# Second bucket pass of a graph-hop kernel: first hop in runs of 3, 3, 3 pairs, three small copies on ScalarE

## The chip, the cores and the metric

One core of one Trainium2 chip. The metric is the device time of one execution in microseconds (us), the median of several runs. One execution was also taken with the hardware profiler; the trace rows below are of that one.

## The reference

N = 10000 nodes, E = 160000 directed edges with random ends, D = 128 features. Seven rounds ("hops") of normalised neighbour sums give eight tokens per node, which then go through one small attention block and a weighted readout.

```python
h = x; toks = [x]
for _ in range(7):
    msg = h[src] * deg_inv_sqrt[src, None] * deg_inv_sqrt[dst, None]
    h = segment_sum(msg, dst, N)
    toks.append(h)
tok = stack(toks, axis=1)                    # (N, 8, D)
# layernorm, self-attention over the 8 tokens, residual, readout softmax -> (N, D)
```

## The kernel before, in words

The 10000 nodes are cut into 79 tiles of 128. A hop multiplies one-hot matrices with the table of node values, so the edges must first be sorted into cells by destination tile and source block. Stages, in order of time: a first bucket pass over the edge list (`pass_a`, to about 400 us of the trace), `decode`, the **second bucket pass** (about 400 to 1160 us), which makes the one-hot matrices tile by tile and runs the first hop with them as they come, then hops 2 to 7 from the stored matrices, then the attention.

The change is in the second bucket pass (`run`, L657 to L725). It goes over 20 groups of four tiles, called quads here (the code's `quads`). In each round of the loop at L706 three generators are advanced in turn, so that their instructions are written out mixed:

- `place(quad q+1)` (L418 to L504), mostly VectorE (DVE) and TensorE (PE). The quad's four tiles are done two at a time: one-hot of the cell keys `oh` (L213), counts on PE (L430, L436) with two ScalarE (ACT) casts `H` and `U` (L431, L438), the product `ux` (L226), ranks `rk` on PE and DVE (L230 to L234), the rank's one-hot `rob` (L213), two products `R` (L219), 50 matmuls `tb` (L449), the cast `tbs` on ACT (L450). Once per quad there follows the overflow part: `dsl` (ACT, L467), `oidx` (L468), `fl`, `ct`, `po`, the overflow ranks `ph` (L483), the digits of the overflowing edges, two one-hots `ohp` (L213) with 16 small matmuls each into `msc` (L496), the copy `lo` of the result (L499), `oidx` again (L502) and `Sov` (L503).
- `matrices(quad q)` (L506 to L536): per tile, rows `rb` and `ra` are fetched from DRAM by the SP queue (L517), and the one-hot tile `w` is built in three parts: L524 on DVE from `rb`, two L529 on ACT from `ra`, L532 on DVE from `dsl`; then `w` is stored to DRAM (`gsd`, L534). `rb` has one buffer, `ra` two, `w` six.
- `hop1(quad q-1)` (L697 to L701) through `block` (L548 to L638): per tile 9 pairs of gathers. One gather is 8 matmuls of 32 columns into a PSUM tile `p` (L608, three buffers); ACT copies it out as `eb` (L613; in the last quad DVE does four of the nine, L615). The copied pair is summed into the PSUM tile `acc` by four matmuls (L558, L559, "scatter"), which are written out two pairs behind the gathers (`lag` is 2). `runs` says how many gathers are written out before the scatters that are due: (2, 2, 2, 3) before. At the tile's end come the two rows of fetched values (`og`, by POOL's indirect DMAs) and a ones column (L566), which close the tile, and then `fin1` (L676): the in-degree `indeg` copied from column 128 of `acc` (L677), `y` and `r` scaled from `acc` on ACT (L680, L651), and every second tile `tab` and `mx`, and the stores.

The order on an engine is not the order of the code alone: a list scheduler in the build reorders each engine's instructions, with the code's order as priority, and sets the semaphores. An engine then runs its list strictly in order. Two buffers matter below: `ux` and `R` share one buffer (tag `ux`, one copy), so the next `ux` waits until `tb` has read `R`; `ohp` and `rob` share one as well.

Of the kernel before, what the change touches and what calls it, by code (L numbers as in the profile page):

```python
# [12 lines left out]
AF = mybir.ActivationFunctionType  # L13
ALU = mybir.AluOpType
# [22 lines left out]
KO = 8  # L37
# [10 lines left out]
class Hops:  # L48
# [369 lines left out]
    def place(self, ts, got):  # L418

        tc, nc, V, A, T, G = self.tc, self.nc, self.nc.vector, self.nc.scalar, self.nc.tensor, self.nc.gpsimd  # L420
        wp, w1, n = self.bwp, self.bw1, len(ts)
# [34 lines left out]
        n, a, b = len(ts), ts[0], ts[-1] + 1  # L456
        msc = self.psm.tile([128, 128], F32, name="msc")
# [12 lines left out]
        n = 4  # L470
# [8 lines left out]
        po = wp.tile([128, 4, 8], F32, name="po")  # L479
        V.tensor_tensor(po[:, :n], msc[:, 0:n, None].to_broadcast([128, n, 8]), self.iof1[:, None, :8].to_broadcast([128, n, 8]), op=ALU.add)  # L480
        V.tensor_mul(po[:, :n], po[:, :n], fl[:, :n])
        ph = wp.tile([128, KO, 4], F16, name="ph")
        V.tensor_scalar(ph.rearrange("p k g -> p g k"), po[:, :n, :KO], -1.0, None, op0=ALU.add)  # L483
        vi = wp.tile([128, 4, 8, 4], I32, name="vi4")
        V.tensor_scalar(vi[:, :n, :, 3], ov[:, :n], -1.0, None, op0=ALU.add)
        V.tensor_single_scalar(vi[:, :n, :, 0], vi[:, :n, :, 3], 14, op=ALU.arith_shift_right)
# [9 lines left out]
                    T.matmul(msc[:, 4 + 3 * (g + i):7 + 3 * (g + i)], ohp[:, k, :, i], dg[:, g + i, k, :], start=k == 0, stop=k == KO - 1)  # L496
        yield
        lo = wp.tile([128, 16], F32, name="lo")
        V.tensor_copy(lo[:, :3 * n], msc[:, 4:4 + 3 * n])  # L499
        l3 = lo[:, :12].rearrange("p (g k) -> p g k", k=3)  # L500
        n = len(ts)
        V.scalar_tensor_tensor(self.oidx[:, a:b, NI], l3[:, :n, 0], 128.0, l3[:, :n, 1], op0=ALU.mult, op1=ALU.add)  # L502
# [154 lines left out]
    def run(self, ctx, att, nhop=K):  # L657
        tc, nc, V, A, T, G = self.tc, self.nc, self.nc.vector, self.nc.scalar, self.nc.tensor, self.nc.gpsimd
        with ExitStack() as c:
            self.bp = c.enter_context(tc.tile_pool(name="bp", bufs=1))  # L660
            self.TT = self.bp.tile([128, NCH, NTP], F32, name="TT")
            G.memset(self.TT[:, :, NK:], 0.0)
            self.pass_a()
            self.decode()
            self.gsp = c.enter_context(tc.tile_pool(name="gs1", bufs=6))
            self.pg = c.enter_context(tc.tile_pool(name="pg1", bufs=3, space=PSUM))
            self.pacc = c.enter_context(tc.tile_pool(name="pc1", bufs=2, space=PSUM))
            self.ogp = c.enter_context(tc.tile_pool(name="og1", bufs=2))
            self.fp = c.enter_context(tc.tile_pool(name="fp1", bufs=1))
            self.pb_open(c)  # L670
            pend = []

            done, stored = [], []


            def fin1(t, s, acc):  # L676
                V.tensor_copy(self.indeg[:, t:t + 1], acc[:, 128:129])  # L677
                if not done:
                    fin1.y = self.fp.tile([128, 2, 128], F32, name="y2")
                A.activation(fin1.y[:, len(done), :], s, AF.Copy, scale=self.dis2[:, t:t + 1])  # L680
                done.append(t)
                self.token_out(1, t, s, self.ctok[0])
                n, b = len(done), t + 1
                if n == 2 or b in (NT, 4 * NG):
                    a, new = b - n, self.tab[1]
                    self.to_table(fin1.y[:, :n, :], new, self.q2, a, b)
                    V.tensor_reduce(self.mx[1][:, a:b], new[:, a:b, 0:128], axis=X, op=ALU.max, apply_absolute_value=True)
                    stored.append((a, b))
                    done.clear()
                    while len(stored) > (t != last1):  # L690
                        self.rows(1, new, *stored.pop(0), nc.sync)


            quads = [list(range(a, min(NT, a + 4))) for a in (*range(4 * NG, NT, 4), *range(0, 4 * NG, 4))]
            dsl, W = [[] for _ in quads], [[] for _ in quads]

            def hop1(q):  # L697
                for t, w in zip(quads[q], W[q]):
                    og = [self.fetch(t, j, (self.tabd[0], self.tabh[0])) for j in range(NI + 1)]
                    yield from self.block(t, w, self.tab[0], og, pend, 2, (2, 2, 2, 3), True,  # L700
                                          lambda jj: q < nq - 1 or jj % 2 == 0, fin1, t == quads[0][0])  # L701

            nq, last1 = len(quads), quads[-1][-1]
            for _ in self.place(quads[0], dsl[0]):
                pass
            for q in range(nq + 1):  # L706
                pl = self.place(quads[q + 1], dsl[q + 1]) if q + 1 < nq else iter(())
                if q == 0:
                    mt = self.matrices(quads[0], dsl[0][0], W[0])
                    next(mt)  # L710
                hp = hop1(q - 1) if q else iter(())
                for i in range(16):
                    if i % 3 != 1:
                        next(pl, None)
                    if i % 4:
                        next(mt, None)
                    next(hp, None)
                for g in (pl, mt, hp):
                    for _ in g:
                        pass  # L720
                if q + 1 < nq:
                    mt = self.matrices(quads[q + 1], dsl[q + 1][0], W[q + 1])
                    next(mt)
            while pend:
                pend.pop(0)()  # L725
        with ExitStack() as c:
# [10 lines left out]
            pend = []  # L737
            for k in range(2, nhop + 1):
                i = 1 - k % 2
# [29 lines left out]
                og = [[None] * (NI + 1) for _ in order]  # L769
# [11 lines left out]
                for n, t in enumerate(order):  # L781
                    w = self.gsp.tile([128, (NJ + NG) * 128], F8, name="w")
# [591 lines left out]
```

## Time and profile before

| | us |
|---|---|
| median of 3 runs | 3912.85 (3900.72 to 3913.69) |
| profiled execution | 3935.55, of which 3933.8 are its span (mean granted TensorE clock 0.977) |
| second bucket pass | about 400 to 1160 of the span |
| the 20 `fl` (L473, one per quad): first start, last start | 403.7, 1099.0 |

The profiled execution is 22.7 us above the median of the runs. In the rows, "x" is a count, a "busy" share is the time in which an engine had an instruction in flight, and [0.88 <-PE tb L449] at a row's end says that the engine stood idle for 0.88 us before the instruction and that the end of PE's L449 released it. Neighbouring instructions of one engine overlap, so what an instruction costs its engine is the step from its start to the next one's start, and not its duration.

### The profile page before, as it was taken

Reading aid. Unit: us, or ns where it says so; the run is one execution under the profiler, and the core shown is the slowest. Engines: PE = TensorE matmul, PEld = TensorE weight load, DVE = VectorE, ACT = ScalarE, POOL = GpSimd, SP = SyncE. Lnnn points to the kernel's source line nnn. Section 1 sums busy time; section 2 is a strip of 40 time slices with the busy share of each in tenths; the row PEclk is TensorE's granted clock in tenths of the full one; section 3 lists DMA queues with packets and bytes.
Section 4 is the critical chain, followed back from the end, with each engine's and each line's share of the span. In section 5 each row is a group of like instructions: output and inputs, shape, how many; then the busy total and the mean of one; then the engine's idle time right before and its main releaser. Section 6 shows DMA issues by size and latency. Waiting matters only on the chain.

```text
span 3933.8 us, 174231 instructions
## 1 busy us (share of the span) xinstructions
PE 3693.9 (94%) x74141; PEld 2983.6 (76%) x74141; DVE 3172.3 (81%) x6888; ACT 2812.9 (72%) x6950; POOL 1678.8 (43%) x2221
## 2 busy tenths in 40 slices
PE   6786899999989999999999999999999998999997
PEld 4665677777768888888788788888878886777775
DVE  8998999999967777777777777777776664888888
ACT  6885577777766666766666667666765667888885
POOL 0000233323236665666666566656656662121111
PEclk8898899999999999999999999999999999999998
DMA  3100454544546666666666666666666552222220
GB/s 101 38 2 1 140 168 154 163 152 161 161 150 202 202 199 194 204 199 204 188 201 201 192 201 203 198 192 199 204 192 201 187 187 92 82 77 85 77 83 19
DMA packets 332729, 595.58 MB, mean 151 GB/s; under 512 B 57447, under 2 KB 215493, under 8 KB 326693
## 3 DMA queue, kind: packets, MB, share of 16 engines
q1 hardware_dynamic: 293989, 506.70, 40.0%
q0 software_dynamic: 35392, 72.55, 6.5%
q8 instruction: 580, 9.50, 1.0%
q10 hardware_dynamic: 2560, 5.12, 0.5%
q14 instruction: 208, 1.70, 0.1%
HBM read 455.49 MB, written 128.67 MB: 148 GB/s over the span
## 4 chain that ended last, share of the span: by engine, by line
PE 75%; DVE 14%; ACT 4%; DMA 4%; issue 2%; SPq 0%; another core or an unknown queue 0%; ACTq 0%; DVEq 0%; POOLq 0%
PE p L608 27%; PE acc L583 23%; PE acc L568 4%; PE pv L1018 4%; PE pu L1002 3%; DVE ux L226 2%; DVE o L219 2%; PE po L1037 2%; PE pt L992 2%; DVE oh L213 2%; PE tb L449 2%; DVE w L532 2%; PE ps L1067 1%; DVE R L219 1%; PE acc L558 1%
## 5 line engine op out<-in xcount | busy, mean ns | idle before, releaser
L613 ACT ACTIVATE eb<-p 128x512 f16<-128x512 f32 x3065 | 1638.7, 603 | 571.0 <-PE p L608 339.1
L615 DVE TENSOR_TENSOR eb<-p,four 128x512 f16<-128x512 f32 x1912 | 1230.9, 685 | 327.5 <-PE acc L583 189.7
L608 PE MATMUL p<-tab,w 128*32 128x256 f16 x39816 | 1291.8, 274 | 39.4 <-ACT eb L613 17.4
L608 PEld LDWEIGHTS <-w 128*32 128x32 fp8e4 x39816 | 997.5, 96 | 223.8 <-issue 169.2
L583 PE MATMUL acc<-eb,w 128*128 128x256 f16 x8532 | 1014.2, 273 | 0.5 <-issue 0.3
L583 PEld LDWEIGHTS <-w 128*128 128x128 fp8e4 x8532 | 836.9, 98 | 99.8 <-issue 1.0
L544 POOL DMA_INDIRECT og<-tabh,oidx x553 | 616.9, 1115 | 655.2 <-DVE oidx L468 394.5
L544 POOL DMA_INDIRECT og<-tabd,oidx x541 | 551.8, 1020 | 739.1 <-PE acc L566 359.6
L653 POOL TENSOR_SCALAR r<-s,ctok 128x128 f32<-128x128 f32 x474 | 294.8, 622 | 44.8 <-DVE s L599 27.8
L644 ACT ACTIVATE tab<-s,c 128x128 f16<-128x128 f32 x395 | 158.5, 401 | 198.0 <-DVE eb L615 171.4
L645 DVE SCALAR_TENSOR_TENSOR tab<-s,c,tab 128x128 f16<-128x128 f32 x395 | 138.9, 352 | 180.9 <-issue 168.3
L1107 POOL TENSOR_TENSOR p<-e,in 128x1024 f32<-128x1024 f32 (+1 forms) x40 | 76.5, 1914 | 446.6 <-DVE e L1106 446.6
L1059 ACT ACTIVATE junk<-tab 128x128 f32<-128x128 f32 x626 | 248.4, 401 | 8.2 <-SPq L1343 6.8
L347 ACT ACTIVATE rs<-iof,rb 128x128 fp8e4<-128x128 f32 x784 | 231.8, 391 | 0.3
L558 PE MATMUL acc<-eb,w 128*128 128x129 f16 x1422 | 214.2, 223 | 1.0 <-ACT w L529 0.9
L532 DVE TENSOR_TENSOR w<-dsl,iof 128x2432 fp8e4<-128x2432 f16 x79 | 211.9, 2682 | 2.7 <-PE acc L559 2.7
L599 DVE TENSOR_REDUCE s<-acc 128x128 f32<-128x256 f32 x474 | 196.3, 414 | 19.9 <-issue 8.9
L559 PE MATMUL acc<-eb,w 128*128 128x128 f16 x1422 | 210.1, 220 | 0.0
L543 POOL COPY og<-eb 128x1 f16<-128x1 f16 x452 | 84.0, 186 | 254.3 <-ACT eb L613 254.3
L558 PEld LDWEIGHTS <-w 128*128 128x128 fp8e4 x1501 | 139.2, 98 | 68.0 <-issue 64.3
L1018 PEld LDWEIGHTS pv<-Wv,xT 128*64 128x64 f32 x2504 | 138.8, 137 | 44.4 <-ACT uT L1003 29.7
L1018 PE MATMUL pv<-Wv,xT 128*64 128x131 f32 x2504 | 163.1, 280 | 8.6 <-issue 3.9
(299 smaller groups left out, 5033.1 us busy)
## 6 DMA issues: line engine op xcount, KB each, us to landing
w<-gsd SPq DMA_DIRECT2D x474, 592.0 KB
gsd<-w SPq DMA_DIRECT2D x79, 592.0 KB
tok<-r SPq DMA_DIRECT2D x546, 64.0 KB
tab<-tok SPq DMA_DIRECT2D x273, 128.0 KB
tabd<-tab SPq DMA_DIRECT2D x396, 64.0 KB
ra<-srow SPq DMA_DIRECT2D x79, 320.0 KB
rb<-srow SPq DMA_DIRECT2D x79, 256.0 KB
og<-tabh,oidx POOLq DMA_INDIRECT x553
```

The source lines that it names most:

```text
L347: A.activation(ro[:, j - a, i, :], self.iof, AF.Abs_reciprocal_sqrt, scale=2.0 ** 21, bias=rb[:, j - VP, i:i + 1], saturate=False)
L532: V.tensor_tensor(w[:, :NJ * 128].rearrange("p (j d) -> p j d", d=128), dsl[:, g, :, None].to_broadcast([128, NJ, 128]), self.iof1[:, None ...
L544: self.nc.gpsimd.indirect_dma_start(out=o, out_offset=None, in_=src[0] if i == NI else src[1], in_offset=bass.IndirectOffsetOnAxis(ap=self ...
L558: T.matmul(acc[0][:, :128 + ones], W, rows[:, 128:256 + ones], start=start, stop=False, skip_group_check=True)
L559: T.matmul(acc[0][:, :128], W, rows[:, :128], start=False, stop=False, skip_group_check=True)
L583: T.matmul(acc[0][:, :256], w[:, J * 128:(J + 1) * 128], e[:, j, :256], start=False, stop=J == NG - 1 and not late)
L608: T.matmul(p[32 * q:32 * q + 32, j], w[:, NJ * 128 + s * CAP:NJ * 128 + (s + 1) * CAP], tab[:, s, :], start=True, stop=True)
L613: A.activation(e[:, :n, 0:256], pv, AF.Copy, scale=4.0)
L615: V.tensor_tensor(e[:, :n, 0:256], pv, self.four[:, :, None].to_broadcast([128, n, 256]), op=ALU.mult)
L653: self.nc.gpsimd.tensor_scalar(r, s, ct[:, t:t + 1], None, op0=ALU.mult)
L1018: T.matmul(p[64 * h:64 * h + 64, u - us[0], :], S[i]["xT"][:, h * m + q, 64 * c:64 * c + 64], Wv, start=True, stop=True, tile_position=(0, ...
L1059: A.activation(j, S[i]["x"][:, g, :], AF.Square, bias=S[i]["x"][:, g, 0:1], scale=-1.0, accum_out=R[i % 6][:, 0, g:g + 1])
```

## The change

Four edits. The overflow ranks `ph` (once per quad), the overflow result `lo` (once per quad) and the in-degree column `indeg` (once per tile) go from DVE to ACT. The first hop's `runs` become (3, 3, 3), so a tile takes three rounds of the mixing loop and not four, and `hop1` is left out in every fourth round, so that it still spreads over the loop's 16.

```diff
-        V.tensor_scalar(ph.rearrange("p k g -> p g k"), po[:, :n, :KO], -1.0, None, op0=ALU.add)
+        A.activation(ph.rearrange("p k g -> p g k"), po[:, :n, :KO], AF.Copy, bias=-1.0)
...
-        V.tensor_copy(lo[:, :3 * n], msc[:, 4:4 + 3 * n])
+        A.copy(lo[:, :3 * n], msc[:, 4:4 + 3 * n])
...
             def fin1(t, s, acc):
-                V.tensor_copy(self.indeg[:, t:t + 1], acc[:, 128:129])
+                A.copy(self.indeg[:, t:t + 1], acc[:, 128:129])
...
-                    yield from self.block(t, w, self.tab[0], og, pend, 2, (2, 2, 2, 3), True,
+                    yield from self.block(t, w, self.tab[0], og, pend, 2, (3, 3, 3), True,
...
-                    next(hp, None)
+                    if i % 4 != 3:
+                        next(hp, None)
```

The lists of the engines are rebuilt by the scheduler, and they change in more places than the diff. Both builds come, after some quads, to a pattern that repeats from quad to quad; it is this pattern that is shown.

**Place 1**, DVE, the overflow part of a quad, from `oidx` (L468) on. Before:

```order
L468 TENSOR_SCALAR oidx<-msc 128x4
L532 TENSOR_TENSOR w<-dsl,iof_228 128x2432
L480 TENSOR_TENSOR po<-msc,iof_228 128x32
L524 TENSOR_SCALAR w<-rb,pid_232 128x1024
L481 TENSOR_TENSOR po<-po,fl 128x32
L483 TENSOR_SCALAR ph<-po 128x4x8
L213 TENSOR_TENSOR ohp<-ph,io_230 128x2048
L677 COPY indeg<-acc 128x1
L532 TENSOR_TENSOR w<-dsl,iof_228 128x2432
L213 TENSOR_TENSOR ohp<-ph,io_230 128x2048
```

The same place on DVE in the changed kernel:

```order
L468 TENSOR_SCALAR oidx<-msc 128x4
L532 TENSOR_TENSOR w<-dsl,iof_228 128x2432
L480 TENSOR_TENSOR po<-msc,iof_228 128x32
L524 TENSOR_SCALAR w<-rb,pid_232 128x1024
L481 TENSOR_TENSOR po<-po,fl 128x32
L532 TENSOR_TENSOR w<-dsl,iof_228 128x2432
L213 TENSOR_TENSOR ohp<-ph,io_230 128x2048
L165 SCALAR_TENSOR_TENSOR tab_65<-y_15189,q_252,tab_65 128x2x128
L687 TENSOR_REDUCE mx_249<-tab_65 128x2
L213 TENSOR_TENSOR ohp<-ph,io_230 128x2048
```

`ph` and `indeg` are gone, the second L532 of the quad stands ahead of the first `ohp` and not behind it, and between the two `ohp` there are now the short `tab` and `mx`. That L532 carries a new wait, for PE's scatters of an older tile whose `w` buffer it overwrites; before, the `indeg` on DVE ahead of it had already waited for the close of that tile or a later one.

**Place 2**, DVE, the middle of the same quad, from `Sov` (L503) to the next `ux` (L226), `R` being two rows. Before:

```order
L503 TENSOR_TENSOR Sov<-lo,iof_228 128x512
L677 COPY indeg<-acc 128x1
L524 TENSOR_SCALAR w<-rb,pid_232 128x1024
L532 TENSOR_TENSOR w<-dsl,iof_228 128x2432
L234 TENSOR_REDUCE rk<-ur 128x50
L213 TENSOR_TENSOR rob<-rk,io_230 128x1600
L452 SCALAR_TENSOR_TENSOR vo<-rk,TT 128x50
L219 TENSOR_TENSOR R<-rob,sl 128x25x64
L219 TENSOR_TENSOR R<-rob,dl 128x25x64
L454 MAX ov<-vo 128x8 x2
L524 TENSOR_SCALAR w<-rb,pid_232 128x1024
L213 TENSOR_TENSOR oh<-kB,io_230 128x3800
```

The same place in the changed kernel:

```order
L503 TENSOR_TENSOR Sov<-lo,iof_228 128x512
L524 TENSOR_SCALAR w<-rb,pid_232 128x1024
L532 TENSOR_TENSOR w<-dsl,iof_228 128x2432
L234 TENSOR_REDUCE rk<-ur 128x50
L524 TENSOR_SCALAR w<-rb,pid_232 128x1024
L213 TENSOR_TENSOR rob<-rk,io_230 128x1600
L452 SCALAR_TENSOR_TENSOR vo<-rk,TT 128x50
L219 TENSOR_TENSOR R<-rob,sl 128x25x64
L219 TENSOR_TENSOR R<-rob,dl 128x25x64
L454 MAX ov<-vo 128x8 x2
L226 TENSOR_TENSOR ux<-oh,U_15812 128x3800
```

The quad's third L524 moved up, from behind `R` to the place right behind `rk`, so only L532 and `rk` are left between it and the L524 ahead. Behind `R` there now comes `ux`, with nothing but the two MAX between; before, L524 and `oh` stood there. Both `oh` (before) and `ux` (now) wait at this place until PE's `tb` has read `R`.

**Place 3**, the SP queue, from the quad's second `rb` load to its third and fourth (L517). `tok` (L655) is the store of `r`, `gsd` (L534) that of `w`, `tabd` (L168) that of `tab`. Before:

```order
L517 DMA rb<-srow 128x1024
L655 DMA tok_66<-r 128x128
L534 DMA gsd_131<-w 128x4736
L517 DMA ra<-srow 128x1280
L168 DMA tabd_167<-tab_65 128x2x256
L517 DMA ra<-srow 128x1280
L655 DMA tok_66<-r 128x128
L517 DMA rb<-srow 128x1024
L534 DMA gsd_132<-w 128x4736
L517 DMA rb<-srow 128x1024
```

The same place in the changed kernel:

```order
L517 DMA rb<-srow 128x1024
L655 DMA tok_66<-r 128x128
L168 DMA tabd_167<-tab_65 128x2x256
L534 DMA gsd_131<-w 128x4736
L517 DMA ra<-srow 128x1280
L655 DMA tok_66<-r 128x128
L517 DMA rb<-srow 128x1024
L534 DMA gsd_132<-w 128x4736
L517 DMA ra<-srow 128x1280
L517 DMA rb<-srow 128x1024
```

The second of the two `ra` loads ahead of the third `rb` load now stands behind it; `gsd`, one `ra` and `tok` are still ahead.

## The prediction

> **What bounds the kernel now.** I read the page first, then windows over the second bucket pass, then who waits for whom in it, then one quad row by row. The page's head has PE in the lead, then DVE:
>
> ```profile
> PE 3693.9 (94%) x74141; PEld 2983.6 (76%) x74141; DVE 3172.3 (81%) x6888; ACT 2812.9 (72%) x6950; POOL 1678.8 (43%) x2221
> ```
>
> That is the whole span; the pass is another matter. These are window rows of PE, PEld, DVE, ACT, POOL, clock, DMA share and GB/s: the middle of the pass, then two slices of 65 us of it, then its tail.
>
> ```profile
> 460.00:1110.00 650.00, 605.05 (x12248) 475.88 (x12247) 602.30 (x894) 498.97 (x1043) 211.88 (x137) 0.99 0.49 159
> 590.00:655.00 65.00, 61.25 (x1260) 49.15 (x1258) 63.57 (x91) 49.48 (x106) 28.53 (x14) 0.97 0.46 150
> 850.00:915.00 65.00, 61.45 (x1268) 48.64 (x1265) 60.05 (x92) 50.44 (x107) 19.19 (x14) 1.00 0.49 158
> 1110.00:1160.00 50.00, 41.98 (x862) 29.29 (x862) 26.57 (x53) 37.94 (x79) 20.45 (x17) 1.00 0.45 133
> ```
>
> DVE and PE are both 93% busy (602.30 and 605.05 of 650), ACT 77%. Early, DVE is full (63.57 of 65); later it stands idle for 5 us in 65. Who makes it wait there (waiting line, releasing line, us in total, times, longest; from 740 to 1110)? And what did ACT wait for in the whole pass (400 to 1160)?
>
> ```profile
> DVE oh L213 <- PE tb L449: 18.6, 17, 1.7
> DVE w L524 <- DMA rb<-srow: 5.2, 8, 1.6
> DVE ux L226 <- ACT U L438: 3.3, 1, 3.3
> ACT eb L613 <- PE p L608: 46.1, 78, 2.6
> ACT y L680 <- DVE indeg L677: 15.9, 23, 1.4
> ```
>
> DVE's waits are for `tb`, which PE can start only when DVE's own `R` is done, and for `rb`, which is fetched only when DVE's own L524 has let its buffer go. So **DVE's list, with the round trips it starts itself, sets the pace**; ACT and PE follow. One quad on DVE (start, duration, line; the last bracket is idle time and its end):
>
> ```profile
> 838.43 2.14 DVE L213 TENSOR_TENSOR oh<-kB,io 128x3800 f16<-128x3800 f16 x1 [0.88 <-PE tb L449]
> ...
> 843.50 0.75 DVE L524 TENSOR_SCALAR w<-rb,pid 128x1024 fp8e4<-128x1024 f16 x1 [0.16 <-DMA rb<-srow]
> 844.17 0.18 DVE L481 TENSOR_TENSOR po<-po,fl 128x32 f32<-128x32 f32 x1
> 844.39 0.20 DVE L483 TENSOR_SCALAR ph<-po 128x32 f16<-128x32 f32 x1
> 844.63 1.23 DVE L213 TENSOR_TENSOR ohp<-ph,io 128x2048 f16<-128x2048 f16 x1
> 845.77 0.15 DVE L677 COPY indeg<-acc 128x1 f32<-128x1 f32 x1
> 845.84 2.68 DVE L532 TENSOR_TENSOR w<-dsl,iof 128x2432 fp8e4<-128x2432 f16 x1
> ...
> 849.57 0.48 DVE L165 SCALAR_TENSOR_TENSOR tab<-y,q,tab 128x256 f16<-128x256 f32 x1
> ...
> 850.44 0.17 DVE L499 COPY lo<-msc 128x12 f32<-128x12 f32 x1
> 850.53 2.13 DVE L226 TENSOR_TENSOR ux<-oh,U 128x3800 f16<-128x3800 f16 x1
> ...
> 853.31 0.74 DVE L524 TENSOR_SCALAR w<-rb,pid 128x1024 fp8e4<-128x1024 f16 x1
> 853.97 2.68 DVE L532 TENSOR_TENSOR w<-dsl,iof 128x2432 fp8e4<-128x2432 f16 x1
> 856.58 0.41 DVE L234 TENSOR_REDUCE rk<-ur 128x50 f16<-128x250 f32 x1
> 857.02 0.99 DVE L213 TENSOR_TENSOR rob<-rk,io 128x1600 f16<-128x1600 f16 x1
> ...
> 859.86 0.27 DVE L454 MAX8 ov<-vo 128x8 f32<-128x25 f32 x2
> 860.58 0.75 DVE L524 TENSOR_SCALAR w<-rb,pid 128x1024 fp8e4<-128x1024 f16 x1 [0.45 <-DMA rb<-srow]
> 862.05 2.14 DVE L213 TENSOR_TENSOR oh<-kB,io 128x3800 f16<-128x3800 f16 x1 [0.72 <-PE tb L449]
> ...
> 875.76 2.14 DVE L213 TENSOR_TENSOR oh<-kB,io 128x3800 f16<-128x3800 f16 x1 [0.91 <-PE tb L449]
> ```
>
> From `oh` at 838.43 to `oh` at 875.76 the quad takes 37.33 us. The overflow's `fl` comes once per quad:
>
> ```profile
> L473 DVE TENSOR_SCALAR fl<-ov x20: 171/180/221, 403.7 to 1099.0; 128x32 f16<-128x32 f32 x20
> ```
>
> That is 695.3 us for 19 quads. By the order of before, 12 of them have the repeating pattern (448 us); the other seven take 247, or 35.3 each. In the changed order the repeating pattern of the front part holds for 11 quads.
>
> **The change part by part, per quad of the pattern.**
>
> *The copies leave DVE.* `indeg` steps from 845.77 to 845.84, 0.07 us; three of four count, since the fourth lies in the wait that ends at 875.76. `ph` steps 0.24 (844.39 to 844.63), `lo` 0.09 (850.44 to 850.53). Sum: **-0.54**. They are cheap there, though their durations read 0.15 to 0.20.
>
> *They go to ACT.* The trace has no such ACT copy; bounds are nothing and, by the nearest row, `dsl`:
>
> ```profile
> L467 ACT CAST dsl<-msc 128x76 f16<-128x76 f32 x18 | 3.9, 218 | 0.4 <-PE msc L465 0.4
> ```
>
> Six copies of 0.22 are 1.3 us per quad. I take nothing: ACT is idle for 151 us of the 650, some 8.5 per quad, and `y` no longer waits for DVE's `indeg` (15.9 us in 23 cases). DVE waits for ACT at `ohp`, behind a 2.6 us L532, and at the `oidx` behind a 2.1 us `ux`; both cover a copy. If that cover were gone, 0.2 to 0.5 each. In the tail ACT is the busy engine (37.94 of 50): a few copies of 0.22, under 1 us.
>
> *The second L532 moves ahead of `ohp` and waits for PE* (place 1). `ohp` and all behind it on DVE stand behind that wait, and PE's `msc` and `tb` wait for those. When is PE there? These are PE rows at that place:
>
> ```profile
> 841.70 1.81 PE L430 MATMUL ur<-oh,id 128*128 128x152 f16 x25
> 843.44 0.62 PE L608 MATMUL p<-tab,w 128*32 128x256 f16 x16
> 843.99 0.23 PE L558 MATMUL acc<-eb,w 128*128 128x129 f16 x1
> 844.06 0.22 PE L559 MATMUL acc<-eb,w 128*128 128x128 f16 x1
> 845.91 0.56 PE L496 MATMUL msc<-dg,ohp 128*128 128x3 f16 x16 [0.41 <-DVE indeg L677]
> ```
>
> Sixteen gathers step 0.55, so a run of three pairs takes 0.83 from 843.44; eight scatters of some 0.06 then end the tile: about 844.95 with the last one's duration. DVE would be at the L532 at 844.27 or so, behind `po`. **+0.7**; bounds 0 (PE earlier by one gather run) and 1.4 (as much later). The second `ohp` needs the first `msc` group read, some 0.14 + 0.56 after the first `ohp`; `tab` and `mx` cover 0.87: **+0.1**, bounds 0 and 0.4.
>
> *The third L524 moves up* (place 2). Before, 853.31 to 860.58 lay between it and the one ahead, now L532 and `rk`: DVE is there at 857.02, 2.97 after the buffer is free at 854.05. How long is a refill? SP issues:
>
> ```profile
> 840.26 0.32 SPq L517 DMA_DIRECT2D rb<-srow  x1
> 854.79 0.38 SPq L517 DMA_DIRECT2D rb<-srow  x1
> ```
>
> The first served the L524 at 843.50 and the second that at 860.58, both ended by that DMA: 3.24 and 5.79 us. So DVE waits at least 0.3 and at most 3.55 (the issue at 854.79 was 0.74 late, held on SP behind `ra` and `tok`). I take **+0.9**, nearer to the short one: by place 3 one of the two `ra` now stands behind the `rb`, and `gsd` goes out earlier.
>
> By the Trainium skill, page "DMA: Bandwidth & Descriptors", section "Anatomy of one DMA — SWDGE (gpsimd) path", a DMA takes about 2.0 us plus its bytes at 436 GB/s. For 256 KB that is an estimate of 2.6 us, by which there would be no wait here and the total below would come out some 10 us lower; it is fitted to another path, and both rows stand above it.
>
> *`ux` takes the wait for `tb`* (place 2). `tb` is read 2.19 us after `R` (859.86 to 862.05). Before, the two MAX (0.18) and L524 (0.66) lay in it, now the MAX alone: **+0.66**. It can't be less unless PE runs `tb` faster, as PE already waits for `R`.
>
> *Runs of 3.* Gathers and scatters are the same in number; what the runs shift shows as the PE wait above. At the tail's end, where PE and ACT set the time, I take nothing; bounds a gather run per tile, 0.5 us for some five tiles, either way.
>
> Sum for such a quad: -0.54 + 0.7 + 0.1 + 0.9 + 0.66 = +1.8 us; 11 of them +20. One quad that was in the pattern and now has `w` work behind `R` instead of a wait: -1.7 (0.54 + 0.45 + 0.72). Seven early quads, where DVE is full and has no such waits: -0.6 each, -4. **Total +14 us**: 3949.6 on the profiled execution's 3935.55. That execution is 22.7 above the median of the runs; I carry the 14 over: 3912.85 + 14 = **3927**.
>
> **The rivals.**
>
> *A, slower by more than 0.5%: the refill of `rb` is a slow one.* Place: the L524 behind `rk`. At 5.79 + 0.74 us after the buffer is free, the wait is 3.55 and not 0.9, 11 x 2.65 = 29 more, or 3956; if the L532 waits 1.4 too, 3964. It decides from 1.4 us of wait, when the sum passes 20. For it: that very load was the slow one of the pattern, and `gsd` still follows it at once. Against: it was held on SP by what now stands elsewhere.
>
> *B, even: the waits stay at their lower ends.* PE is at the L532 in time, `rb` comes in 3.24: -0.54 + 0 + 0 + 0.3 + 0.66 = +0.4 per quad, 11 x 0.4 - 5.7 = -1, or 3912. The DMA page's rule named above leads here. For it: PE waited for DVE in the row at 845.91. Against: in the rows above PE needs until about 844.5 for that tile even with sixteen gathers, and DVE is there at 844.27.
>
> *C, faster by more than 0.5%: DVE's pace was set through ACT.* If ACT's 15.9 us of waiting for `indeg` had held up the gathers, and these DVE, all of it comes back, and with 20 x 0.54 that is -27, or 3886. Against it: DVE waited for ACT just 3.3 us in the rows above.
>
> The Trainium skill, page "Perfetto Trace Analysis", section "Optimizing Scalar/DVE Operations", leads to a smaller C: about 125 ns on DVE per PSUM operation and 60 per SBUF one, and moving work to ScalarE pays where DVE is saturated. By it 99 PSUM copies and 20 others would give an estimate of 13.6 us; the steps above, 0.07 and 0.09 for the PSUM copies, say less.
>
> *D, it does less than it says.* Excluded for the copies, which are off DVE's list; in the built list of PE three gathers stand in a row where there were two.
>
> **How the numbers follow.** Forecast (waits near what I took; 3918 to 3940) 0.50; A 0.26; B 0.16; C 0.08. A difference of 0.5%, 20 us here, is about what a measurement of this kernel can tell from no change. The forecast lies beyond +20 us (3932.5) with a fifth of its chance. Slower by over 0.5%: 0.26 + 0.10 = 0.36; faster: C, 0.08, and a little of B, 0.10; the same: 0.54. The range leaves out C and A's upper part: from 3900 to 3955.
>
> **What would show it.** In the changed trace: `ux` waiting for `tb` some 2 us in about 11 quads; L524 waiting for `rb` some 10 us in all, at the one behind `rk`; L532 waiting for PE's L559 some 8; `y` no more for `indeg`; 39 us from one `oh` behind a wait to the next quad's. Wrong if DVE waits no more than before in the pass, or if ACT or PE is named as what holds `ohp` and `oidx`.

## The result, and the profile after

The changed kernel takes 3921.34 us (median of 9 runs, 3918.03 to 3933.38), the kernel before 3912.37, measured beside it (9 runs). The ratio over all runs is 1.0032, with a 95% interval of 1.0023 to 1.0041: slower by some 12.5 us (the two medians alone are 9.0 apart), and by less than 0.5%. The forecast was 3927, or +14 us. The profiled execution took 3918.73 us, of which 3916.9 are its span.

The head of the page, in the same order of engines as before:

```profile
PE 3688.0 (94%) x74141; PEld 2992.6 (76%) x74141; DVE 3152.8 (80%) x6769; ACT 2773.4 (71%) x7069; POOL 1703.9 (44%) x2221
```

DVE has 119 instructions less (79 + 20 + 20) and ACT 119 more. That span is 17 us *shorter* than the one of before, although the median is longer; where is that? `s` (L599) is a reduction in hops 2 to 7, which no edit touches, and `fl` is the once-per-quad mark of the pass. The rows of the changed kernel, then of the kernel before:

```profile
L599 DVE TENSOR_REDUCE s<-acc x474: 409/414/426, 1184.4 to 3265.0; 128x128 f32<-128x256 f32 x158
L473 DVE TENSOR_SCALAR fl<-ov x20: 174/181/182, 400.0 to 1113.7; 128x32 f16<-128x32 f32 x20
```

```profile
L599 DVE TENSOR_REDUCE s<-acc x474: 408/414/425, 1175.5 to 3282.9; 128x128 f32<-128x256 f32 x158
```

The hops last 2080.6 us in one execution and 2107.4 in the other. The pass itself is longer: its 20 `fl` span 713.7 us against 695.3, and the hops start at 1184.4 against 1175.5. So the gain of the span lies in code that did not change, and the loss in the pass.

The ten quads from the ninth `fl` to the nineteenth are in the repeating pattern in both kernels (the first of the ten of before still differs from the others in the order of a few instructions). Window rows (PE, PEld, DVE, ACT, POOL, clock, DMA share, GB/s), first of the changed kernel, then of the one before:

```profile
683.00:1076.00 393.00, 353.81 (x7145) 283.28 (x7143) 341.02 (x455) 296.89 (x670) 139.47 (x81) 0.97 0.48 152
```

```profile
685.00:1062.00 377.00, 350.57 (x7141) 275.82 (x7141) 348.71 (x517) 292.21 (x611) 115.16 (x82) 1.00 0.49 158
```

DVE works 7.7 us less in ten quads and yet takes 16 us longer. A list of waits over the same windows says why, again after and before:

```profile
DVE ux L226 <- PE tb L449: 21.7, 10, 3.4
DVE w L524 <- DMA rb<-srow: 19.9, 17, 3.3
DVE oh L213 <- PE tb L449: 9.0, 10, 0.9
```

```profile
DVE oh L213 <- PE tb L449: 21.9, 20, 1.7
DVE w L524 <- DMA rb<-srow: 4.3, 8, 1.6
```

That is 50.6 us of waits instead of 26.2, or +24.4; less the 7.7 of work, it is the 16 within 1 us. And one ordinary quad of the changed kernel on DVE, from `oh` behind a wait to the next such `oh`, 38.66 us:

```profile
884.33 2.14 DVE L213 TENSOR_TENSOR oh<-kB,io 128x3800 f16<-128x3800 f16 x1 [0.88 <-PE tb L449]
...
890.02 0.20 DVE L481 TENSOR_TENSOR po<-po,fl 128x32 f32<-128x32 f32 x1
890.15 2.68 DVE L532 TENSOR_TENSOR w<-dsl,iof 128x2432 fp8e4<-128x2432 f16 x1
892.75 1.21 DVE L213 TENSOR_TENSOR ohp<-ph,io 128x2048 f16<-128x2048 f16 x1
...
894.62 1.22 DVE L213 TENSOR_TENSOR ohp<-ph,io 128x2048 f16<-128x2048 f16 x1
895.76 2.13 DVE L226 TENSOR_TENSOR ux<-oh,U 128x3800 f16<-128x3800 f16 x1
897.81 0.16 DVE L502 SCALAR_TENSOR_TENSOR oidx<-lo 128x4 int32<-128x4 f32 x1
...
898.48 0.75 DVE L524 TENSOR_SCALAR w<-rb,pid 128x1024 fp8e4<-128x1024 f16 x1
...
901.75 0.41 DVE L234 TENSOR_REDUCE rk<-ur 128x50 f16<-128x250 f32 x1
903.80 0.75 DVE L524 TENSOR_SCALAR w<-rb,pid 128x1024 fp8e4<-128x1024 f16 x1 [1.64 <-DMA rb<-srow]
...
909.55 2.14 DVE L226 TENSOR_TENSOR ux<-oh,U 128x3800 f16<-128x3800 f16 x1 [1.98 <-PE tb L449]
...
922.99 2.14 DVE L213 TENSOR_TENSOR oh<-kB,io 128x3800 f16<-128x3800 f16 x1 [0.92 <-PE tb L449]
```

Both waits of place 2 stand where the prediction put them: L524 behind `rk`, and `ux` behind `R`. The L532 at 890.15, which was to wait for PE, follows `po` without a wait.

### The profile page after: what moved, and what is told of

Its sections match the earlier page's. It is cut to its first block, busy times and chain, and to the rows that moved or that the text cites. A ratio compares the mean times of both kernels' runs of the same rounds, so it can differ in the third digit from the quotient of the medians.

```text
span 3916.9 us, 174241 instructions
## 1 busy us (share of the span) xinstructions
PE 3688.0 (94%) x74141; PEld 2992.6 (76%) x74141; DVE 3152.8 (80%) x6769; ACT 2773.4 (71%) x7069; POOL 1703.9 (44%) x2221
## 4 chain that ended last, share of the span: by engine, by line
PE 65%; DMA 2%; DVE 1%; ACT 1%; issue 0%; SPq 0%; POOL 0%; ACTq 0%; POOLq 0%; DVEq 0%
PE p L608 24%; PE acc L583 23%; PE pv L1019 4%; PE acc L568 4%; PE pu L1003 3%; PE po L1038 2%; PE pt L993 2%; PE ps L1068 1%; DMA og<-tabd,oidx 1%; PE pf L1227 1%; PE sm L1074 1%; PE pf L1053 0%; ACT junk L1060 0%; DMA tabd<-tab 0%; DMA ogl<-tabd,oidx 0%
## 5 line engine op out<-in xcount | busy, mean ns | idle before, releaser
L613 ACT ACTIVATE eb<-p 128x512 f16<-128x512 f32 x3065 | 1586.1, 607 | 568.7 <-PE p L608 548.3
L615 DVE TENSOR_TENSOR eb<-p,four 128x512 f16<-128x512 f32 x1912 | 1190.5, 683 | 306.0 <-PE p L608 300.3
L608 PE MATMUL p<-tab,w 128*32 128x256 f16 x39816 | 1272.8, 275 | 14.6 <-ACT eb L613 4.9
L583 PEld LDWEIGHTS <-w 128*128 128x128 fp8e4 x8532 | 834.9, 98 | 97.6 <-issue 0.8
L544 POOL DMA_INDIRECT og<-tabh,oidx x553 | 627.8, 1135 | 611.4 <-DVE oidx L468 404.3
L544 POOL DMA_INDIRECT og<-tabd,oidx x541 | 565.9, 1046 | 582.7 <-PE acc L559 361.3
L645 DVE SCALAR_TENSOR_TENSOR tab<-s,c,tab 128x128 f16<-128x128 f32 x395 | 169.2, 428 | 180.5 <-ACT tab L644 180.1
L532 DVE TENSOR_TENSOR w<-dsl,iof 128x2432 fp8e4<-128x2432 f16 x79 | 211.9, 2683 | 0.5 <-PE acc L559 0.4
L599 DVE TENSOR_REDUCE s<-acc 128x128 f32<-128x256 f32 x474 | 196.5, 415 | 14.6 <-PE acc L597 11.1
L558 PEld LDWEIGHTS <-w 128*128 128x128 fp8e4 x1501 | 142.8, 99 | 51.0 <-issue 48.7
L559 PEld LDWEIGHTS <-w 128*128 128x128 fp8e4 x1501 | 148.9, 99 | 36.0 <-issue 34.4
```

The source lines that it names most:

```text
L532: V.tensor_tensor(w[:, :NJ * 128].rearrange("p (j d) -> p j d", d=128), dsl[:, g, :, None].to_broadcast([128, NJ, 128]), self.iof1[:, None ...
L544: self.nc.gpsimd.indirect_dma_start(out=o, out_offset=None, in_=src[0] if i == NI else src[1], in_offset=bass.IndirectOffsetOnAxis(ap=self ...
L558: T.matmul(acc[0][:, :128 + ones], W, rows[:, 128:256 + ones], start=start, stop=False, skip_group_check=True)
L559: T.matmul(acc[0][:, :128], W, rows[:, :128], start=False, stop=False, skip_group_check=True)
L583: T.matmul(acc[0][:, :256], w[:, J * 128:(J + 1) * 128], e[:, j, :256], start=False, stop=J == NG - 1 and not late)
L608: T.matmul(p[32 * q:32 * q + 32, j], w[:, NJ * 128 + s * CAP:NJ * 128 + (s + 1) * CAP], tab[:, s, :], start=True, stop=True)
```

## The experiments

The theory: DVE's list sets the pace; the edits themselves save a little, and what costs is where the scheduler then puts the third L524 and `ux`. The rival: the edits cost by themselves, the copies by way of ACT, the runs by PE's order. Ratios are to the kernel before, whose runs were taken beside each group of kernels; in the four groups its medians were 3912.4, 3943.5, 3909.3 and 3908.9, so times of different groups aren't compared. "Period" is the mean of the ten quads from the ninth to the nineteenth `fl`, and "work" DVE's busy time in it.

| kernel | ratio | interval | period, us | work | idle |
|---|---|---|---|---|---|
| before | 1 | | 37.63 | 34.80 | 2.83 |
| before, once more | (one execution) | | 37.53 | 34.78 | 2.75 |
| the change | 1.0032 | 1.0023 to 1.0041 | 39.26 | 34.07 | 5.20 |
| copies alone | 1.0033 | 1.0022 to 1.0044 | 39.39 | 34.29 | 5.11 |
| runs alone | 1.0030 | 1.0019 to 1.0040 | 38.73 | 34.60 | 4.13 |
| the change, third L524 put back | 0.9989 | 0.9980 to 0.9998 | 37.82 | 34.20 | 3.62 |
| the change, two `rb` buffers | 1.0020 | 1.0009 to 1.0030 | 38.07 | 33.98 | 4.09 |
| copies alone, third L524 put back | 0.9986 | 0.9976 to 0.9997 | 38.08 | 34.49 | 3.60 |
| `ph` and `lo` alone | 0.9981 | 0.9972 to 0.9991 | 38.10 | 34.34 | 3.76 |
| the change, covers behind `R`, two `rb` | 0.9977 | 0.9967 to 0.9987 | 38.21 | 33.99 | 4.22 |
| three edges, two `rb`: no edit | 0.9974 | 0.9964 to 0.9985 | 37.15 | 34.72 | 2.43 |
| the same, with the runs | 0.9985 | 0.9972 to 0.9998 | 37.21 | 34.48 | 2.73 |
| the same, with the copies | 1.0009 | 0.9999 to 1.0019 | 38.23 | 34.26 | 3.97 |
| the same, with both | 1.0001 | 0.9992 to 1.0010 | 38.14 | 34.05 | 4.09 |

Work differs by less than 0.9 us, idle time by up to 2.8. The period alone doesn't give the time: four kernels (third L524 put back, twice; `ph` and `lo` alone; covers behind `R`) have a longer period than before and a shorter time. The ratio comes from 8 to 12 runs, the period from one execution, and that one can lie at the end of the runs: with two `rb` buffers it was the shortest of twelve, with covers the longest of eleven. So the periods and waits below say where a kernel waits, and the ratios what it costs.

**The kernel before, once more.**

> The kernel before, unchanged, in one more profiled execution beside the runs of this call. In the first profiles the end of the second bucket pass lies 8.9 us later in the changed kernel, but its hops 2 to 7, which no edit touches, are 27 us shorter. If that is the execution's or the chip's and not the kernel's, the hops (first s of hop 2 to first s of hop 8) take as long here as in the experiments already taken (2085 us in each) and unlike the first profile of before (2084) by no more than a few us; the fl rows span 695 us again, within 3. If the fl rows span 5 us more or less than that, the differences of a single execution are too large for arguments of 10 us.

```profile
L599 DVE TENSOR_REDUCE s<-acc x474: 409/414/426, 1173.2 to 3254.8; 128x128 f32<-128x256 f32 x158
L473 DVE TENSOR_SCALAR fl<-ov x20: 169/181/217, 403.7 to 1101.3; 128x32 f16<-128x32 f32 x20
```

The pass repeats (697.6 us, from 695.3). The hops don't, and that figure was missed: from the first `s` to the last the same kernel takes 2081.6 us here and 2107.4 in its first profile. So the 27 us don't belong to the change. In the fourteen profiles this stretch has two sizes: 2080 to 2087 us in nine, 2107 to 2117 in five, which are the first one of before and the four taken beside the median of 3943.5. Beside this second profile of before, the changed kernel's span is 10.5 us longer (3916.9 and 3906.4), and its hops start 11.2 us later (1184.4 and 1173.2). Nearly the whole loss lies ahead of the hops.

**One part alone.** The copies without the runs, and the runs without the copies:

> The three copies on ScalarE, the runs left at 2, 2, 2, 3. Theory L (the loss comes from where the build puts L524, behind rk, and from what stands behind R): in this build's list L524 is behind rk as well and behind R only the two MAX come before the wait for tb, so the refill wait of about 1.6 us and the tb wait of about 2 us per quad are both there in some 10 quads: 3915 to 3925, as with the whole change. Rival R (the runs of 3 cost the time): the copies alone save DVE 20 x 0.54, so 3900 to 3906. Rival M (the copies are slow on ScalarE): above 3925, with DVE waiting for ScalarE at ohp and oidx.

> The runs of 3 alone, the three copies on VectorE. Theory L: L524 stands behind R as in the kernel before, so there is no refill wait behind rk and DVE's idle time per quad stays near 2.5 us: 3907 to 3915 (the kernel before is at 3912). Rival R (the runs of 3 cost the time): 3918 to 3925, with PE or ScalarE named as what DVE waits for.

Each part alone costs as much as both (1.0033 and 1.0030). For the runs that is a miss of the theory as it was put. But the waits differ. Over the ten quads of the copies alone, then of the runs alone:

```profile
DVE oh L213 <- PE tb L449: 25.4, 19, 2.3
DVE w L524 <- DMA rb<-srow: 19.8, 17, 2.5
```

```profile
DVE ux L226 <- PE tb L449: 12.7, 5, 3.7
DVE oh L213 <- PE tb L449: 8.9, 10, 0.9
DVE w L524 <- DMA rb<-srow: 8.2, 15, 1.8
DVE ux L226 <- issue: 7.3, 5, 2.1
```

The copies alone move the third L524 behind `rk` (rb 19.8, as in the whole change), and `oh` stays behind `R`. The runs alone come to an order of two quads in turn: in one, that L524 stays behind `R` and `ux` follows it; in the other it stands ahead of `oidx`, and `ux` follows `R` with the two MAX alone between. In neither is it behind `rk` (rb 8.2). So the two halves of place 2 come from different edits.

**The third L524 put back**, by an edge that only orders DVE's list, in the whole change and in the copies alone:

```diff
-            self.times(R[:, :, CAP:], ro, cols(self.dl))
+            lastR = self.times(R[:, :, CAP:], ro, cols(self.dl))
+            if p0 == 0:
+                self.r0 = lastR
...
-            V.tensor_scalar(w[:, cut:], rb, self.pid1, 0.25, op0=ALU.is_equal, op1=ALU.mult, saturate=False)
+            i524 = V.tensor_scalar(w[:, cut:], rb, self.pid1, 0.25, op0=ALU.is_equal, op1=ALU.mult, saturate=False)
+            if g == 2:
+                self.after(i524, self.r0)
```

> The whole change, and one ordering edge more: the quad's third L524 is queued behind the second R, where the kernel before has it. Theory L: the refill wait (1.6 us per quad) goes, and 0.66 of the tb wait is covered again; 11 quads x 2.3 = 25 us less than the changed kernel: 3890 to 3902, below the kernel before. Rivals R and M: the place of L524 does not matter, 3916 to 3926.

> Only the three copies on ACT (runs 2, 2, 2, 3), and the quad's third L524 put back on DVE's list behind the second R, where the kernel before has it. In the copies alone (ratio 1.0033) this L524 stood behind rk, as in the whole change. Theory (the list of the engine, not the copies, costs the time): rb waits fall from 26.8 us to under 16, the tb waits from 27 to about 24, and the time falls to the kernel before or below it, ratio 0.996 to 1.000. Rival (the copies themselves cost, since ohp and oidx now wait for ACT and ACT has more to do): the ratio stays at 1.002 to 1.004, with ACT named in DVE's waits for ten us or more.

The ten quads of the first, then of the second (the edge's lines shift the numbers, L529 is L524 and L454 is L449):

```profile
DVE oh L213 <- PE tb L454: 22.2, 20, 1.8
DVE w L529 <- DMA rb<-srow: 7.7, 9, 2.1
```

```profile
DVE oh L213 <- PE tb L454: 21.7, 20, 2.7
DVE w L529 <- DMA rb<-srow: 4.5, 7, 1.7
```

With that instruction back in its place both are below the kernel before: -0.43% and -0.47%, or 17 and 18 us, against the same kernel without the edge. For the whole change the theory had 25, so it was a miss in size. The scheduler also moves more than the edge names: in both lists the second L532 stands between the two `ohp` again, as in the kernel before, and `ux` goes behind `Sov`. In the lists without the edge these two hardly waited, but their moves were not tested apart. In the whole change the edge brings `oh` back behind `R` as well, so it undoes both halves of place 2; in the copies alone `oh` had stayed there, and the L524 half is the only one undone.

**Two `rb` buffers**, so that the refill is no longer waited for. In the built list the third L524 then stands still further up, right behind the second, and `ux` stays behind `R`:

```diff
-        vi = wp.tile([128, 4, 8, 4], I32, name="vi4")
+        vi = wp.tile([128, 4, 8, 4], I32, name="vi4", bufs=1)
...
-            rb = self.bw1.tile([128, 4 * NG * CAP - m], F16, name="rb")
+            rb = self.bw1.tile([128, 4 * NG * CAP - m], F16, name="rb", bufs=2)
```

> The whole change, with two buffers for rb (and one for vi4, to make room), so that a refill no longer waits for the L524 ahead. Theory L: DVE's waits for the rb DMA go from 33 us in the pass to under 6; the wait for tb at ux stays at about 2 us per quad: 3895 to 3906. Rival: the time shifts from one wait into the other, because PE or ScalarE sets the pace: 3916 to 3926 with a longer wait for tb.

```profile
DVE ux L226 <- PE tb L449: 22.8, 10, 2.9
...
DVE ohp L213 <- PE msc L496: 5.8, 4, 2.5
DVE w L524 <- DMA rb<-srow: 2.0, 5, 1.0
```

In the pattern the rb waits fall by 18 us and the period by 1.2 us a quad, as the theory has it. That already counts the 5.8 us that come up at `ohp`. The whole gains only 0.12%, some 5 us and not 15 to 26, and the two intervals overlap: the time is the rival's, although the wait for `tb` hardly grew (31.9 us from 30.7). The first eight quads are slower by 3 us in all (35.75 each, 35.35 in the change); where the rest of the gain went isn't shown. So the waits bear the theory out here, and the time doesn't.

**`ph` and `lo` alone**, a build whose list keeps the third L524 behind `R` without any edge:

> Only ph and lo on ACT (indeg stays on DVE, runs 2, 2, 2, 3). In this build's list the third L524 stays behind R, as in the kernel before. Theory (list order): no new wait for rb or tb; 0.33 us less of DVE per quad, 20 quads, -6 us at most: ratio 0.997 to 1.000. Rival (ACT's copies in the chain ohp - msc - lo - oidx hold DVE up): 1.001 or more, and DVE waits for ph and lo by more than 5 us.

0.9981, some 7 us less, about what it takes off DVE (6.6). Yet DVE waits 7.8 us for `lo` in the ten quads, so the rival's wait is there too. Where the gain lies isn't shown: in the two profiles taken beside each other the hops start at 1173.0 here and at 1173.2 in the kernel before.

**Covers behind `R`.** With two `rb` buffers as well, edges set the L532 of the third and fourth tile behind the two `R`:

```diff
+            if g == 2 and self.r0:
+                self.after(i532, self.r0)
+            if g == 3 and self.r2:
+                self.after(i532, self.r2)
```

> The whole change, with two order edges on DVE's list (the L532 of the quad's third tile behind the first pair's R, the L532 of the fourth behind the second pair's) and two rb buffers (vi4 with one, for room). Each R is then followed by 2.6 us of w work before oh, which reads what tb gives 2.2 us after R; both tb waits and the rb waits should go. Theory (DVE's waits set the pace): some 4.5 us of waits per quad in 11 quads fall to 1 or less; against the kernel before, which waits 2.5, it is 1.5 less, and 0.5 less of copies, 2 us in 11 to 16 quads: ratio 0.991 to 0.995. Rival (PE or ACT is so near behind that DVE's gain is lost to waits for them): 0.997 to 1.001, with DVE waiting for acc, msc, eb or ph instead.

```profile
DVE rk L235 <- PE ur L232: 27.8, 20, 2.6
```

No `tb` wait is left, and a new one has its size: with L532 gone from between `ux` and `rk`, DVE waits there for PE's `ur` in all 20 cases. The theory's 0.991 to 0.995 was missed; the rival was right in the number (0.9977) and wrong in the place.

**The list held.** A third edge sets the L532 of the second tile behind the first `ux`. Its four kernels, with none of the edits, the runs, the copies, and both, have nearly the same DVE list, but not quite: with the copies the first L532 stands ahead of both `po` and not behind them, and with the runs the third L524 is back behind `rk`:

```diff
+            if g == 1 and self.ux0:
+                self.after(i532, self.ux0)
```

> None of the four edits, but three order edges on DVE's list (the L532 of a quad's second tile behind the first pair's ux, that of the third behind the first pair's R, that of the fourth behind the second pair's R) and two rb buffers. The same edges go on the other three kernels of this call, so that the four lists are nearly alike and what the edits themselves are worth can be read without a moved list. By the trace of the run with covers behind R alone, each R is now followed by 2.6 us of work where 2.2 is needed, the first ux by 2.6 where 2.1 is needed; left are some 0.6 at the second rk, 0.7 between the two ohp, 0.4 at the second oidx, 1.7 us of waits per quad where the kernel before has 2.6. Theory (DVE's waits set the pace): 12 to 15 quads by 0.9, -11 to -13 us, ratio 0.996 to 0.998. Rival (PE and ACT are next and take most of it): 0.999 to 1.001.

> As the run with no edit but the order edges, and the runs of 3, 3, 3 with the skipped round. Alone and with a free list they cost +0.30%. Theory (the cost was the list: ux directly behind R): with the list held they are worth nothing, within 0.1% of the run with edges alone. Rival (runs of 3 themselves cost, by PE's order of gathers and scatters): 0.2 to 0.4% above the run with edges alone, with PE's scatters or gathers named in DVE's or ACT's waits.

> As the run with no edit but the order edges, and the three copies on ACT. Alone and with a free list they cost +0.33%. Theory (the cost was the list: the third L524 behind rk): with the list held they are worth what they take off DVE, 0.54 to 0.7 us per quad, 20 quads, so 0.2 to 0.35% below the run with edges alone. Rival (DVE now waits for ACT's ph and lo as long as it saved): even with the run with edges alone, within 0.1%, and more than 10 us of waits for ph and lo.

> The whole change with the order edges and two rb buffers. Theory: the sum of the two parts, 0.2 to 0.35% below the run with edges alone, ratio to the kernel before 0.993 to 0.996, and below the change as it is by 0.7 to 1.0%. Rival (the edits cost something that has nothing to do with DVE's list): not below the run with edges alone.

The kernel with no edit came as expected and has the lowest ratio, 0.9974: it beats both the kernel before and the changed one. The runs cost +0.11% against it, with overlapping intervals, where they cost 0.30% with a free list: most of that looks to have been the list, but the difference isn't measured finely enough to rule the rival's 0.2% out. The copies were a miss: +0.35% with these edges, about what they cost with the free list, and so was the change as a whole, +0.27%. The largest new wait is at the second `oidx`. DVE with `lo` on DVE (L508 there), then DVE, ACT and PE with `lo` on ACT:

```profile
987.95 1.22 DVE L214 TENSOR_TENSOR ohp<-ph,io 128x2048 f16<-128x2048 f16 x1 [0.65 <-PE msc L505]
...
989.87 0.17 DVE L508 COPY lo<-msc 128x12 f32<-128x12 f32 x1
990.08 0.16 DVE L511 SCALAR_TENSOR_TENSOR oidx<-lo 128x4 int32<-128x4 f32 x1
```

```profile
963.20 1.23 DVE L214 TENSOR_TENSOR ohp<-ph,io 128x2048 f16<-128x2048 f16 x1 [0.65 <-PE msc L505]
...
966.07 0.16 DVE L511 SCALAR_TENSOR_TENSOR oidx<-lo 128x4 int32<-128x4 f32 x1 [0.98 <-ACT lo L508]
```

```profile
964.52 0.56 PE L505 MATMUL msc<-dg,ohp 128*128 128x3 f16 x16
```

```profile
965.14 0.83 ACT L538 ACTIVATE w<-ra,off 128x640 fp8e4<-128x640 f16 x1
965.86 0.17 ACT L508 COPY lo<-msc 128x12 f32<-128x12 f32 x1
```

`msc` is complete at 965.08, and ACT takes `lo` at 965.86, behind an L538 (the L529 of before) that stands ahead of it in ACT's list and starts at 965.14. The copy itself is 0.17 us; the queue ahead of it costs 0.7. From `ohp` to `oidx` it is 2.13 us without the copy on DVE and 2.87 with it on ACT. In these edged lists only a 0.66 us L524 lies in that gap; in the change a 2.1 us `ux` does, and there `oidx` at 897.81 doesn't wait. Over the ten quads DVE's listed waits are 38.8 us with the copies and 21.8 with no edit. Two of them only the former has; the second may in part be an exchange, as the wait of `tab` for ACT, two instructions ahead of a `rk`, falls from 6.0 to 2.1:

```profile
DVE oidx L511 <- ACT lo L508: 8.9, 10, 1.5
DVE rk L235 <- PE ur L232: 6.8, 12, 0.9
```

So `oidx` accounts for about half of the 17 us. The moved L532 is a rival that these four kernels don't separate.

## Why the prediction was right

Per quad of the pattern the forecast was +1.8 us, and +1.63 was measured (39.26 - 37.63). But two of its terms didn't come, and two were larger.

- **Copies off DVE, -0.54.** DVE's busy time falls by 0.73; the copies alone give 0.51, the runs alone 0.20. Right for what it named.
- **Copies on ACT, nothing.** Right in the ten quads of the change, where no wait of DVE for ACT is listed. The cover that the step named, the `ux` ahead of `oidx`, is there; in the list with three edges, without it, the wait is the 0.98 above (0.89 on average), more than the 0.2 to 0.5 that I gave for lost cover, since I had priced a copy and not the ACT queue ahead of it. PE, which the step left out, waits longer for ACT's `eb`: over the ten quads, after and before,

```profile
PE acc L558 <- ACT eb L613: 18.9, 15, 3.5
```

```profile
PE p L608 <- ACT eb L613: 6.9, 13, 0.7
```

  With the copies alone such waits are 21.1 us, with the runs alone 16.6. They don't show in DVE's waits of the ten quads.
- **The second L532 waits for PE, +0.7.** This step failed: it didn't wait in the ten quads. I had taken PE's times from the rows of before, where the gathers start 5.01 us behind `oh`. In the changed kernel PE stands as follows:

```profile
886.62 1.67 PE L430 MATMUL ur<-oh,id 128*128 128x152 f16 x23
888.23 0.84 PE L608 MATMUL p<-tab,w 128*32 128x256 f16 x24
...
889.90 0.22 PE L559 MATMUL acc<-eb,w 128*128 128x128 f16 x1
```

  The gathers start 3.90 behind `oh` (888.23 - 884.33), and the last scatter of the tile ends at 890.12, just as DVE comes from `po`. The 0.84 for a run of three was right, its start was 1.1 us early. The chance that I gave to PE being in time, as an end of the range, was the case.
- **The second `ohp`, +0.1.** No wait there; `tab` and `mx` cover it, as worked out.
- **The third L524, +0.9.** It waits in all ten quads, from 0.85 to 3.31 us, 15.4 in all: +1.5, between the ends 0.3 and 3.55. The refill took 3.54 to 4.20 us from issue to use in nine of the ten, longer than the short row (3.24) that I chose, and in four of the ten it was held on SP for 0.9 to 1.5 more, behind `tok` in the quad above:

```profile
899.68 0.32 SPq L655 DMA_DIRECT2D tok<-r  x1
900.10 0.38 SPq L517 DMA_DIRECT2D rb<-srow  x1
```

  The buffer was free at 899.23, the load was issued at 900.10 and used at 903.80. In the tenth (863.79) 6.21 us lay between issue and use, rival A's case, once. The estimate of 2.6 us from the Trainium skill, page "DMA: Bandwidth & Descriptors", section "Anatomy of one DMA — SWDGE (gpsimd) path", which led to rival B, stands below all of these; the trace doesn't agree.
- **`ux` takes the `tb` wait, +0.66.** 2.17 us on average over the ten, against 1.32 at the `oh` of before that stood there: +0.85.

Their sum as measured, -0.73 + 1.5 + 0.85, is 1.6. So the total was near for a reason that is partly luck: 0.8 that didn't come stood against 0.8 that came on top. Two smaller steps failed as well. The early quads were to gain 4 us. The eight ahead of the window lose 1.2 against the first profile of before (35.35 and 35.20 each) and gain 1.1 against the second (35.49): DVE wasn't full in them, and its idle time there is 18 us, from 14 and 16. And the pass starts 3.7 us earlier (`fl` at 400.0), which I hadn't looked at. The prediction also held that 0.5% is about what a measurement of this kernel can tell from no change; the interval here is 0.1% to either side.

Rival C is out: ACT's wait of `y` for `indeg` is gone from the changed trace, and no kernel with that copy gained more than some 9 us (0.9977) of C's 27. The Trainium skill, page "Perfetto Trace Analysis", section "Optimizing Scalar/DVE Operations", gave an estimate of 13.6 us for moving the copies; with the third L524 put back, the three gave some 5 us (0.9986); with the free list (1.0033) and with the three edges (+0.35%) they cost time instead.

What stays open: why the first eight quads differ by up to 1.3 us each from list to list was not taken apart, nor why each part alone costs as much as both. "List held" is about the order on DVE alone, and only nearly; PE's and ACT's lists were left to the scheduler. The theory that the edits themselves cost nothing fell for the copies. The reading that fits the runs is that a moved copy costs or gains by what lies between its producer and its reader on DVE; no run varied that alone.

## What to carry to other kernels

Where an engine's list sets the pace and it waits for round trips that it starts itself (a refill, a product that reads its last result), look in the built order at what stands in each such gap: this change saved 0.7 us of work per quad and added 2.4 of waits, nearly all of it in two gaps that lost their cover. In these runs the price of a copy moved to another engine fits the queue it joins and the work left between its producer and its reader, not by its own 0.2 us. And place work into gaps in the list only after checking which gap it is taken from: covering both `R` gaps opened the `ux` one at almost the same price.

## What the hardware showed that I hadn't expected

The granted clock of PE fell to half in the changed kernel's ten quads, in five places, where the kernel before has no stretch of 4 us below 0.95 (both kernels have such falls ahead of the ten quads). In four of the five PE had stood idle for ACT's `eb`, for 3.47, 1.61, 1.18 and 1.12 us, until at most 2.2 us before the fall. Eight other idle waits of 1.2 to 1.6 us in the ten quads had no fall behind them, so the length of a wait alone doesn't decide. The fifth place is the one that reached DVE: after the long rb wait DVE's `R` was late, PE stood idle, and its next 50 matmuls went slowly (PE's rows of that place and of an ordinary one, then window rows of PE busy, clock, DMA share, GB/s):

```profile
867.43 3.40 PE L449 MATMUL tb<-R,oh 128*76 128x64 f16 x50 [2.55 <-DVE R L219]
...
907.43 2.02 PE L449 MATMUL tb<-R,oh 128*76 128x64 f16 x50 [0.37 <-DVE R L219]
```

```profile
864.00:867.40 3.40, 0.88 (x20) 1.00 0.48 152
867.40:871.00 3.60, 3.57 (x58) 0.53 0.29 114
```

The same 50 matmuls take 3.40 and 2.02 us, so one late refill is paid twice: 3.31 us at L524, and 1.4 more at the `ux` behind it (3.36 instead of 1.98). The Trainium skill, page "TensorE: Matmul & The Clock Gate", section "Part 1: The HAM clock gate (the "warmup" mystery)", has the clock fall to half after an idle window of about 3.4 us. The half agrees (0.53 over 3.6 us). The idle time before the fall was 2.55 us here, and between 1.12 and 1.61 us in three of the other four places, shorter than the page gives; only the 3.47 reaches it.
